# Summing the halves of an attention product in a later matmul, with another order on ScalarE and other steps for K

## The chip, the cores and the metric

The kernel runs on one core of one Trainium2 chip. The metric is the device time of one execution in microseconds (us), as a median over runs. The core's engines are TensorE (PE in the profile; PEld is its stream of weight loads), VectorE (DVE), ScalarE (ACT), GpSimd (POOL) and SyncE (SP), which here issues DMAs.

## What is computed

Three layers in a row, all in float32. The first is attention over pooled queries, the second a mixture of experts, the third a product with a cosine. The change lies in the first:

```
q, k, v: (2, 8, 1152, 64)
q_pool = q.reshape(B, H, S // 2, 2, D).mean(axis=3)
scores = scale * np.matmul(q_pool, k.transpose(0, 1, 3, 2))
scores = scores - np.max(scores, axis=-1, keepdims=True)
attn = np.exp(scores)
attn = attn / (np.sum(attn, axis=-1, keepdims=True) + 1e-09)
x = np.matmul(attn, v)          # then transposed to (1152 tokens, 512)
logits = x @ w_gate             # and x @ w_noise, top 2 of 8 experts
```

## The kernel before

Products of float32 are made from rounded high parts and the rest (low parts), as several matmuls of the type fp32r. The 8 heads are taken in 4 pairs (hp), a pair has two heads (hl), and a head has 9 tiles of 128 queries (t); over both batches these are 72 tiles, numbered n = 18 hp + 9 hl + t. In a tile, t = 4 holds queries of both batches.

The loop at L764 emits the work of all engines tile by tile, and each engine runs its own instructions in that order. In tile n:

- PE makes the scores of tile n + 1 in three banks of PSUM called s (s_mm, L285), from K tiles (kt, kb) and query tiles (q, l, qd).
- DVE reads the three maxima of n + 1 (s_max, L293), ACT the three exps (s_exp, L300), which write one tile p of three parts.
- PE transposes p of tile n in three groups (t_pe, L314) into banks called pt, of which there are three. ACT copies the first two as high parts eh (t_hi), DVE subtracts for the low parts el (t_lo). The third group ACT copies as it is to rw (t_pool, L339), and GpSimd makes eh and el of it.
- PE works off a queue of attention-value products (avq, L350): a group g of 2 or 3 token tiles (256 or 320 columns) takes 18 matmuls into the one bank pa. V stands in the weights as 64 high and 64 low columns, so rows 0 to 63 of pa hold the product with the high part, rows 64 to 127 that with the low part. NPOP (L761) says how many matmuls a tile takes; each group ends with the last of some tile.
- When a group has ended, fold_a (L367) lets ACT copy one half of pa to the other head's place, ft, and fold_b (L373) in the next tile, behind the first maximum, lets DVE add the other half to it: xt, with both heads of the pair, one below the other.
- For a pair's second head, fold_b also puts x_group (L606) in a list (fill). It is taken at the end of a tile that has no q_group or k_group: per token tile one matmul of xt with 160 columns of GW, an identity of 128 columns beside 32 columns of gate weights. That turns x token-major and gives its share of the logits. DVE then scales both (LGP, L620; X, L637), and SP writes X to memory (x_d, L640).

The steps of the next pair's K and Q are placed by plan (L642), a table of tile numbers: load_k, three k_group (PE transposes, ACT copies to st), k_split (GpSimd, high part sh and rest st) and k_asm (six DMAs from SP that put kt and kb together), each for both batches. m is the first tile of the pair ahead and d is 1 for the first such pair, else 0. The second batch of K is first needed by the scores of a pair's tile 4. SP issues its DMAs in order, so that one which waits holds up all behind it. At the start of a tile its planned steps come first, those of q_group and k_group last.

Behind the last tile come the rest of the products, the last x_groups and the routing of tokens (L842 ff.), then the experts.

Of the kernel before, what the change touches and what calls it, by code (L numbers as in the profile page):

```python
# [22 lines left out]
def attn_moe_cos_kernel(ctx, tc, q, k, v, w_gate, w_noise, noise, w1, w2, w_in, w_out, out):  # L23
# [27 lines left out]
    GW = xp.tile([128, 2, 192], F32, name="GW")  # L51
# [13 lines left out]
    def load_gate():  # L65
        nc.gpsimd.memset(GW, 0.0)
        for a in range(2):
            nc.gpsimd.tensor_scalar(GW[:, a, 32:160], ident, 1.0, 0.0, op0=OP.mult, op1=OP.add)
        for hl in range(2):
            rs = slice(hl * 64, hl * 64 + 64)  # L70
            for o in range(2):
                c = 160 * o + 16 * hl
                for i, w in enumerate((w_gate, w_noise)):
                    nc.sync.dma_start(GW[rs, :, c + 8 * i:c + 8 * i + 8],
                                      w.rearrange("(a o h d) e -> o h d a e", o=2, h=2, d=64)[o, hl])
# [238 lines left out]
    def t_pe(n, j):  # L314
        last = n == NTOT - 1 and j == 0
        TB[n, j] = p = ps.tile([128, 512], F32, name="s", bufs=4) if last else tbank()
        src = P[n].rearrange("p a b -> p (a b)")
        for i in range(3):
            c = 3 * j + i
            nc.tensor.transpose(p[:, i * 128:(i + 1) * 128], src[:, c * 128:(c + 1) * 128], ident)  # L320
# [25 lines left out]
    avq, fold, FT = [], [], {}  # L346
# [20 lines left out]
    def fold_a():  # L367
        hp, hl, g, p, w = fold[0]
        tmp = FT[0] = sb.tile([128, 320], F32, name="ft", bufs=2)
        me, ot = slice(hl * 64, hl * 64 + 64), slice(64 - hl * 64, 128 - hl * 64)  # L370
        nc.scalar.activation(tmp[me, 0:w], p[ot, 0:w], AF.Copy)

    def fold_b():  # L373
        hp, hl, g, p, w = fold.pop(0)
        b, lo, hi = GR[g]
        me = slice(hl * 64, hl * 64 + 64)
        if hl == 0 and g == 0:
            XT[hp] = sb.tile([128, N], F32, name="xt", bufs=1)
        nc.vector.tensor_tensor(XT[hp][me, lo:hi], p[me, 0:w], FT[0][me, 0:w], op=OP.add)  # L379
# [226 lines left out]
    def x_group(hp, g):  # L606
# [3 lines left out]
        lo, xo = (0, 32) if hp % 2 == 0 else (128, 0)  # L610
# [3 lines left out]
        pv = p[:, 0:160 * nt].rearrange("p (i c) -> p i c", c=160)  # L614
# [4 lines left out]
        def x_logits():  # L619
            nc.vector.tensor_tensor(LGP[:, ts, LGS[hp]:LGS[hp] + 2, :],  # L620
                                    pv[:, :, lo:lo + 32].rearrange("p i (h e) -> p i h e", h=2),
# [3 lines left out]
        x_mul = lambda: x_store(hp, ts, pv[:, :, xo:xo + 128], ri)  # L625
# [16 lines left out]
    def plan():  # L642
# [5 lines left out]
        for hp in range(HP):  # L648
# [6 lines left out]
            if hp:  # L655
# [108 lines left out]
    for n in range(NTOT):  # L764
# [57 lines left out]
        if fill and not fl:  # L822
# [21 lines left out]
    if avq:  # L844
        fold_a()
        fold_b()
# [4 lines left out]
    fold_a()  # L851
# [635 lines left out]
```

## Time and profile before

| what | value |
|---|---|
| three timed runs | 813.6, 813.65, 817.45 us, median 813.65 |
| the profiled execution | 812.25 us |
| its span, first to last instruction | 810.4 us |
| busy, share of the span | PE 94%, PEld 86%, DVE 77%, ACT 66%, POOL 49% |
| mean granted clock of PE | 0.977 |

The profile is of one execution. Busy shares are over the whole span; the attention takes the first 290 us or so, and its limits are read there. Times within the trace count from the span's start. A wait is put down to the engine that came last before it ended. PE and PEld are shown apart: matmuls run one behind the other and their ends are modelled, so a matmul record is longer than the step from one to the next.

### The profile page before, as it was taken

How to read it: one execution, taken by the hardware profiler on the slowest of the kernel's cores; microseconds unless marked ns; L12 is line 12 of the kernel's file. 1: busy time of each engine (PE TensorE's matmuls, PEld its weight loads, DVE VectorE, ACT ScalarE, POOL GpSimd, SP SyncE). 2: the span in 40 equal slices, each digit the busy share in tenths (PEclk: the TensorE clock that was granted, in tenths of full speed). 3: DMA queues.
4: the chain of work that ended last, by engine and by line, in shares of the span. 5: the costliest groups of instructions: out<-in, count | busy, mean ns of one | idle time of the engine just before them, and what ended most of it. 6: DMA issues, size and time to landing. Idle time of an engine off the chain costs nothing.

```text
span 810.4 us, 14005 instructions
## 1 busy us (share of the span) xinstructions
PE 765.7 (94%) x4915; PEld 700.7 (86%) x4915; DVE 627.7 (77%) x1240; ACT 534.4 (66%) x1257; POOL 397.1 (49%) x358
## 2 busy tenths in 40 slices
PE   7899999989999989899999999999978999999996
PEld 4699899979899879889999999999876899999995
DVE  5578878867888987459999999987689777685663
ACT  5799889869979884355555555645466666575553
POOL 4767777667867857406557656466055211000000
PEclk8999999999999999989999999999989999999999
DMA  9829769896864104977978979887433111000001
GB/s 206 180 64 201 179 155 240 222 243 138 205 136 143 59 8 170 326 230 246 322 253 308 317 257 337 275 311 225 169 100 116 53 53 27 30 24 28 1 0 43
DMA packets 90141, 133.64 MB, mean 165 GB/s; under 512 B 26928, under 2 KB 57008, under 8 KB 90064
## 3 DMA queue, kind: packets, MB, share of 16 engines
q1 hardware_dynamic: 83664, 111.17, 48.9%
q0 software_dynamic: 5392, 18.48, 6.3%
q10 hardware_dynamic: 1008, 3.02, 1.4%
q8 instruction: 41, 0.67, 0.3%
q14 instruction: 36, 0.29, 0.1%
HBM read 81.20 MB, written 29.88 MB: 137 GB/s over the span
## 4 chain that ended last, share of the span: by engine, by line
PE 58%; DVE 13%; DMA 9%; ACT 8%; issue 5%; POOL 5%; SPq 0%; ACTq 0%; DVEq 0%; POOLq 0%
PE h L977 19%; PE acc L977 12%; PE acc L1008 7%; PE pa L358 6%; PE s L280 6%; PE pt L320 5%; DMA kt<-st 4%; ACT p L304 3%; DVE u L563 2%; DMA qn<-in_q_dram 1%; POOL xg_d L529 1%; ACT u L562 1%; PE t L969 1%; DVE cn L1297 1%; POOL st L227 1%
## 5 line engine op out<-in xcount | busy, mean ns | idle before, releaser
L296 DVE TENSOR_REDUCE nm<-s 128x1 f32<-128x384 f32 x216 | 110.4, 550 | 48.0 <-PE s L280 32.3
L304 ACT ACTIVATE p<-s,nm 128x384 f32<-128x384 f32 x216 | 123.7, 584 | 10.1 <-DVE nm L298 8.8
L977 PE MATMUL h<-xe,u 128*128 128x320 f32 x768 | 126.0, 313 | 0.0
L977 PEld LDWEIGHTS h<-xe,u 128*128 128x128 f32 x768 | 114.1, 188 | 2.1
L1064 POOL TENSOR_SCALAR raw<-raw 128x1024 f32<-128x1024 f32 x16 | 66.0, 4124 | 94.5 <-ACT raw L1063 90.2
L563 DVE TENSOR_TENSOR u<-raw,u 128x1024 fp32r<-128x1024 f32 x66 | 88.7, 1348 | 19.7 <-ACT u L562 19.5
L320 PE MATMUL pt<-ident,p 128*128 128x128 f32 x645 | 98.9, 278 | 1.9 <-ACT rw L341 1.1
L280 PE MATMUL s<-kt,q 128*128 128x384 f32 x240 | 84.2, 371 | 10.5 <-DMA kt<-st 6.4
L358 PE MATMUL pa<-eh,v 128*128 128x320 f32 (+1 forms) x279 | 87.9, 330 | 1.6 <-DVE xt L379 0.9
L320 PEld LDWEIGHTS pt<-ident,p 128*128 128x128 f32 x645 | 78.3, 142 | 10.8 <-ACT rw L341 5.8
L977 PE MATMUL h<-x,u 128*128 128x256 f32 (+1 forms) x576 | 87.0, 302 | 0.0
L977 PEld LDWEIGHTS h<-x,u 128*128 128x128 f32 x576 | 83.4, 195 | 3.7 <-DVE cr L1304 0.4
L562 ACT ACTIVATE u<-raw 128x1024 fp32r<-128x1024 f32 x73 | 76.8, 1057 | 8.1 <-DMA raw<-w_d 5.0
L358 PE MATMUL pa<-el,v 128*128 128x320 f32 (+1 forms) x279 | 81.5, 307 | 0.0
L333 ACT ACTIVATE eh<-pt 128x384 fp32r<-128x384 f32 x144 | 63.3, 494 | 24.9 <-PE pt L320 23.7
L1008 PE MATMUL acc<-hh,u 128*128 128x320 f32 x448 | 76.4, 313 | 0.0
L337 DVE TENSOR_TENSOR el<-pt,eh 128x384 fp32r<-128x384 f32 x144 | 73.3, 549 | 2.7 <-ACT eh L333 1.0
L344 POOL TENSOR_TENSOR el<-rw,eh 128x384 fp32r<-128x384 f32 x71 | 71.7, 1011 | 5.9
L1008 PEld LDWEIGHTS acc<-hh,u 128*128 128x128 f32 x448 | 68.7, 190 | 0.1
L977 PE MATMUL acc<-u,gh 128*128 128x512 f32 x216 | 68.6, 399 | 0.0
L343 POOL TENSOR_SCALAR eh<-rw 128x384 fp32r<-128x384 f32 x71 | 36.4, 512 | 65.4 <-ACT rw L341 58.8
L1082 POOL DMA_INDIRECT g<-y_d,ROWC x18 | 20.3, 1129 | 96.8 <-DVE cm L1090 67.5
(237 smaller groups left out, 1719.7 us busy)
## 6 DMA issues: line engine op xcount, KB each, us to landing
raw<-in_moe_w_dram SPq DMA_DIRECT2D x64, 512.0 KB, 5.9
raw<-in_moe_w_in_dram SPq DMA_DIRECT2D x16, 512.0 KB, 4.6
raw<-in_moe_w_out_dram SPq DMA_DIRECT2D x16, 512.0 KB, 7.2
w_d<-dw POOLq DMA_DIRECT2D x16, 512.0 KB, 6.5
raw<-w_d SPq DMA_DIRECT2D x14, 512.0 KB, 4.2
xg_d<-ZERO SPq DMA_DIRECT2D x10, 512.0 KB, 5.9
vn<-in_v_dram SPq DMA_DIRECT2D x16, 288.0 KB, 5.0
q<-sh SPq DMA_DIRECT2D x14, 304.0 KB, 4.4
```

The lines of the kernel that those rows point to most:

```text
L280: nc.tensor.matmul(o, l, r, start=(m == 0), stop=(not lo and m == len(mm) - 1))
L296: nc.vector.tensor_reduce(NM[n][:, i:i + 1], SB[n][i][:, 0:384], axis=AX.X, op=OP.max, negate=True)
L304: nc.scalar.activation(P[n][:, i], SB[n][i][:, 0:384], AF.Exp, bias=NM[n][:, 3:4], accum_out=SUMS[:, t, 2 * hp + hl, i:i + 1])
L320: nc.tensor.transpose(p[:, i * 128:(i + 1) * 128], src[:, c * 128:(c + 1) * 128], ident)
L337: nc.vector.tensor_tensor(el, t_src(n, j), ef, op=OP.subtract)
L344: nc.gpsimd.tensor_tensor(el, rw, ef, op=OP.subtract)
L358: nc.tensor.matmul(st["p"][:, 0:w], V2[hp, hl, b][:, c, :], (EH, EL)[s][:, c, EB[g]:EB[g] + w], start=(c == 0 and s == 0), stop=(c == 8 an ...
L562: nc.scalar.activation(b[:, 0], r, AF.Copy)
L563: st_w["lo"].tensor_tensor(b[:, 1], r, b.bitcast(F32)[:, 0], op=OP.subtract)
L977: nc.tensor.matmul(o, l, r, start=first and i == 0, stop=last and i == len(seq) - 1)
L1008: nc.tensor.matmul(ACC[e, d][:, 0:CAP], w[:, i, 128 * d:128 * d + 128], r, start=f == 0 and r is hh and i == 0, stop=f == 7 and r is hl)
L1064: nc.gpsimd.tensor_scalar(m, m, 2.0 ** -15, 0.0, op0=OP.is_ge, op1=OP.add)
```

## The change

- fold_a and fold_b become one step, fold_x: DVE copies all 128 rows of pa to xt, a tile of its own for each head (two buffers), in the same tile n, behind t_lo. ACT copies no ft any more. The step stands before the tile's x_group, so a group can now be folded and turned in one tile.
- x_group makes two matmuls per token tile, one for each head, of 80 columns. GW holds the 64-wide identity twice, in rows 0 to 63 and 64 to 127, so that the matmul adds the halves; the gate weights stand twice too.
- p is three tiles of four buffers in place of one of two. ACT's rw comes before the third exp.
- K: the second and third k_group of the first batch, its split, load and assembly, and the third k_group of the second batch, its split and assembly come one tile earlier (for the first such pair only those of the second batch).
- In the last tile no x_group is taken from the list.

```diff
-    GW = xp.tile([128, 2, 192], F32, name="GW")
+    GW = xp.tile([128, HP, 96], F32, name="GW")
...
     def load_gate():
-        nc.gpsimd.memset(GW, 0.0)
-        for a in range(2):
-            nc.gpsimd.tensor_scalar(GW[:, a, 32:160], ident, 1.0, 0.0, op0=OP.mult, op1=OP.add)
...
+        for hp in range(HP):
+            for h in range(2):
+                c = slice(64 * h, 64 * h + 64)
+                nc.gpsimd.tensor_scalar(GW[c, hp, 16:80], ident[c, c], 1.0, 0.0, op0=OP.mult, op1=OP.add)
...
         if i == 0:
-            P[n] = sb.tile([128, 3, 384], F32, name="p", bufs=2)
-        nc.scalar.activation(P[n][:, i], SB[n][i][:, 0:384], AF.Exp, bias=NM[n][:, 3:4],
+            P[n] = []
+        P[n].append(sb.tile([128, 384], F32, name="p", bufs=4))
+        nc.scalar.activation(P[n][i], SB[n][i][:, 0:384], AF.Exp, bias=NM[n][:, 3:4],
...
-    def fold_a():
-        hp, hl, g, p, w = fold[0]
-        tmp = FT[0] = sb.tile([128, 320], F32, name="ft", bufs=2)
-        me, ot = slice(hl * 64, hl * 64 + 64), slice(64 - hl * 64, 128 - hl * 64)
-        nc.scalar.activation(tmp[me, 0:w], p[ot, 0:w], AF.Copy)
-
-    def fold_b():
+    def fold_x():
         hp, hl, g, p, w = fold.pop(0)
         b, lo, hi = GR[g]
-        me = slice(hl * 64, hl * 64 + 64)
-        if hl == 0 and g == 0:
-            XT[hp] = sb.tile([128, N], F32, name="xt", bufs=1)
-        nc.vector.tensor_tensor(XT[hp][me, lo:hi], p[me, 0:w], FT[0][me, 0:w], op=OP.add)
+        if g == 0:
+            XT[hp, hl] = sb.tile([128, N], F32, name="xt", bufs=2)
+        nc.vector.tensor_copy(XT[hp, hl][:, lo:hi], p[:, 0:w])
         if hl == 1:
             fill.append(lambda: x_group(hp, g))
...
         for i, t in enumerate(tl):
-            nc.tensor.matmul(p[:, 160 * i:160 * i + 160], XT[hp][:, t * 128:(t + 1) * 128],
-                             GW[:, hp // 2, 32 - xo:192 - xo], start=True, stop=True)
...
+            for hl in range(2):
+                c = 160 * i + 80 * hl
+                nc.tensor.matmul(p[:, c:c + 80], XT[hp, hl][:, t * 128:(t + 1) * 128],
+                                 GW[:, hp, 16 * hl:16 * hl + 80], start=True, stop=True)
...
                 for j in range(3):
-                    at(m + (8 + d, 10, 11)[j], k_group, hp, 0, j)
-                at(m + 12, k_split, hp, 0)
-                at(m + 12, load_k, hp, 1)
-                at(m + 13, k_asm, hp, 0)
+                    at(m + (8 + d, 9 + d, 10 + d)[j], k_group, hp, 0, j)
+                at(m + 11 + d, k_split, hp, 0)
+                at(m + 11 + d, load_k, hp, 1)
+                at(m + 12 + d, k_asm, hp, 0)
                 for j in range(3):
-                    at(m + (14, 15, 17)[j], k_group, hp, 1, j)
-                at(m + 18, k_split, hp, 1)
-                at(m + 19, k_asm, hp, 1)
+                    at(m + (14, 15, 16)[j], k_group, hp, 1, j)
+                at(m + 17, k_split, hp, 1)
+                at(m + 18, k_asm, hp, 1)
...
         if nx:
             s_mm(n + 1)
-            s_max(n + 1, 0)
-        if fold:
-            fold_b()
-        if nx:
-            s_max(n + 1, 1)
-        if nx:
-            s_max(n + 1, 2)
+            for i in range(3):
+                s_max(n + 1, i)
...
         if fold:
-            fold_a()
+            fold_x()
         if nx:
+            t_pool(n, 2)
             s_exp(n + 1, 2)
-            t_pool(n, 2)
...
-        if fill and not fl:
+        if fill and not fl and nx:
             fill.pop(0)()
```

Three places show how the instructions move. The first is PE in tile n = 12, where the product of the first token group of a pair's second head ends; rows are in PE's order, s are scores of the next tile, GW the matmuls of x_group. Before:

```order
L358 MATMUL pa<-el,v_606 128x256
L280 MATMUL s<-kt,q_279 128x384
L280 MATMUL s<-kt,l_282 128x384
L280 MATMUL s<-kt,q_279 128x384
L280 MATMUL s<-kt,l_282 128x384
L280 MATMUL s<-kt,q_279 128x384
L280 MATMUL s<-kt,l_282 128x384
L320 MATMUL pt<-ident,p 128x128 x9
L612 MATMUL pa<-GW,xt 128x160 x2
```

Now:

```order
L358 MATMUL pa<-el,v_623 128x256
L606 MATMUL pa<-GW,xt 128x80 x4
L280 MATMUL s<-kt,q_281 128x384
L280 MATMUL s<-kt,l_284 128x384
L280 MATMUL s<-kt,q_281 128x384
L280 MATMUL s<-kt,l_284 128x384
L280 MATMUL s<-kt,q_281 128x384
L280 MATMUL s<-kt,l_284 128x384
L320 MATMUL pt<-ident,p 128x128 x9
```

The matmuls of x_group stand directly behind the product that they read, a tile earlier. The same holds in eight places in all: for the first token group of each pair, for the last one of the first three pairs, and for the second one of the last pair.

The second place is SP's queue where the third pair of heads begins (n = 36), with the DMAs that put together the second batch of K. Before:

```order
L640 DMA x_d<-X 128x2x128
L154 DMA l_2348<-ql 64x1216 x2
L162 DMA qd<-ql 64x128 x2
L425 DMA xg_d<-ZERO 128x2x512
L640 DMA x_d<-X 128x3x128
L237 DMA kt<-sh 64x1152
L239 DMA kb<-sh 64x1152
L240 DMA kt<-st 64x1152
```

Now:

```order
L634 DMA x_d<-X 128x2x128
L154 DMA l_2416<-ql 64x1216 x2
L162 DMA qd<-ql 64x128 x2
L237 DMA kt<-sh 64x1152
L239 DMA kb<-sh 64x1152
L240 DMA kt<-st 64x1152
```

The pieces of kt stand ahead of the write of X of the third token group (128x3x128), and directly behind l and qd. The write of X ahead of these is that of the second group, whose x_group is now taken one tile later.

The third place is ACT in two tiles of the attention in which a k_group is copied (st). Before, with a fold in the second of them:

```order
L333 ACTIVATE eh<-pt 128x3x128 x2
L304 ACTIVATE p,SUMS<-s,nm 128x384 x2
L371 ACTIVATE ft<-pa 64x256
L304 ACTIVATE p,SUMS<-s,nm 128x384
L341 ACTIVATE rw<-pt 128x384
L171 ACTIVATE st<-pt 128x384
```

Now:

```order
L333 ACTIVATE eh<-pt 128x3x128 x2
L305 ACTIVATE p,SUMS<-s,nm 128x384 x2
L341 ACTIVATE rw<-pt 128x384
L305 ACTIVATE p,SUMS<-s,nm 128x384
L171 ACTIVATE st<-pt 128x384
```

The copy to ft is gone, and rw stands before the third exp.

## Rows read from the trace of the kernel before

**Rows 1.** Busy time by stretch: from:to, length, PE, PEld, DVE, ACT, POOL, PEclk, DMA share, GB/s.

```profile
90.00:120.00 30.00, 28.54 (x204) 26.42 (x203) 23.68 (x56) 26.15 (x82) 23.52 (x26) 1.00 0.80 194
...
150.00:180.00 30.00, 26.38 (x179) 24.70 (x178) 21.39 (x53) 22.16 (x66) 20.17 (x25) 0.94 0.97 230
180.00:210.00 30.00, 29.67 (x217) 28.39 (x217) 23.53 (x57) 28.44 (x87) 21.84 (x24) 1.00 0.76 168
```

**Rows 2.** Waits, 35 to 290 us: engine, line <- waited for: us in total, times, longest.

```profile
PEld s L280 <- ACT p L304: 6.5, 21, 0.5
PEld pt L320 <- ACT rw L341: 5.8, 17, 0.6
...
PE s L280 <- DMA kt<-st: 4.7, 3, 3.3
...
PEld pt L612 <- DVE el L337: 1.4, 3, 0.5
PE pt L320 <- ACT rw L341: 1.1, 4, 0.4
...
PE s L280 <- ACT p L304: 0.9, 5, 0.2
PE pa L358 <- DVE xt L379: 0.9, 2, 0.6
...
PE pt L612 <- DVE el L337: 0.8, 3, 0.3
PE pa L358 <- DVE X L637: 0.7, 1, 0.7
```

**Rows 3.** The chain that ended last, 150 to 173 us: start, us, what.

```profile
164.34 7.12 DMA kt<-st
...
171.60 1.44 PE s L280 x6
```

**Rows 4.** Busy time by stretch behind that wait, columns as in rows 1.

```profile
172.00:174.00 2.00, 2.00 (x11) 1.90 (x10) 1.39 (x3) 0.00 (x0) 1.75 (x3) 0.66 0.95 208
174.00:176.00 2.00, 2.00 (x11) 2.00 (x10) 1.47 (x4) 1.50 (x5) 0.00 (x0) 0.50 1.26 250
```

**Rows 5.** SP's DMA issues, 150 to 173 us: start, us, queue, line, what, count.

```profile
153.70 0.37 SPq L640 DMA_DIRECT2D x_d<-X  x1
...
155.32 2.39 SPq L162 DMA_DIRECT2D qd<-ql  x2
...
161.86 0.37 SPq L640 DMA_DIRECT2D x_d<-X  x1
162.33 1.27 SPq L237 DMA_DIRECT2D kt<-sh  x1
```

**Rows 6.** Groups of instructions by line and form: count | busy us, mean ns | idle before.

```profile
L379 DVE TENSOR_TENSOR xt<-pa,ft 64x320 f32<-64x320 f32 x16 | 7.7, 484 | 0.3
L371 ACT ACTIVATE ft<-pa 64x320 f32<-64x320 f32 x17 | 7.3, 432 | 0.7 <-PE pa L358 0.3
...
L379 DVE TENSOR_TENSOR xt<-pa,ft 64x256 f32<-64x256 f32 x15 | 6.3, 418 | 0.8 <-ACT ft L371 0.5
...
L1018 DVE COPY yt<-acc 128x320 f32<-128x320 f32 x14 | 6.1, 476 | 0.5 <-PE acc L1008 0.5
```

**Rows 7.** Weight loads in order of time, 84 us: start, us, what, count.

```profile
84.10 0.19 PEld L358 LDWEIGHTS pa<-eh,v 128*128 128x128 f32 x1
84.21 0.19 PEld L358 LDWEIGHTS pa<-el,v 128*128 128x128 f32 x1
...
84.80 0.61 PEld L612 LDWEIGHTS pt<-GW,xt 128*128 128x128 f32 x4
```

**Rows 8.** Matmuls in order of time at the end of a product, 70 us: columns as in rows 7.

```profile
70.19 0.28 PE L358 MATMUL pa<-el,v 128*128 128x256 f32 x1
70.31 0.33 PE L280 MATMUL s<-kt,q 128*128 128x384 f32 x1
```

**Rows 9.** DVE in order of time behind the x_group of that product: columns as in rows 7.

```profile
74.56 0.41 DVE L637 TENSOR_TENSOR X<-pa,RINV 128x256 f32<-128x256 f32 x1
```

More of the change, by code (lines that the diff above doesn't have):

```diff
@@ L65, in load_gate @@
     def load_gate():
-        nc.gpsimd.memset(GW, 0.0)
-        for a in range(2):
-            nc.gpsimd.tensor_scalar(GW[:, a, 32:160], ident, 1.0, 0.0, op0=OP.mult, op1=OP.add)
[L69 to L72, printed above, removed]
+        for hp in range(HP):
+            for h in range(2):
+                c = slice(64 * h, 64 * h + 64)
+                nc.gpsimd.tensor_scalar(GW[c, hp, 16:80], ident[c, c], 1.0, 0.0, op0=OP.mult, op1=OP.add)
+        for half in range(2):
+            rs = slice(half * 64, half * 64 + 64)
+            for h in range(2):
                 for i, w in enumerate((w_gate, w_noise)):
-                    nc.sync.dma_start(GW[rs, :, c + 8 * i:c + 8 * i + 8],
-                                      w.rearrange("(a o h d) e -> o h d a e", o=2, h=2, d=64)[o, hl])
+                    c = 80 * h + 8 * i
+                    nc.sync.dma_start(GW[rs, :, c:c + 8], w.rearrange("(a h d) e -> h d a e", h=2, d=64)[h])
     QB1 = 640
@@ L316, in t_pe @@
         TB[n, j] = p = ps.tile([128, 512], F32, name="s", bufs=4) if last else tbank()
-        src = P[n].rearrange("p a b -> p (a b)")
         for i in range(3):
-            c = 3 * j + i
-            nc.tensor.transpose(p[:, i * 128:(i + 1) * 128], src[:, c * 128:(c + 1) * 128], ident)
+            c = slice(i * 128, i * 128 + 128)
+            nc.tensor.transpose(p[:, c], P[n][j][:, c], ident)
     def t_dst(n, j):
@@ L344, in t_pool @@
         nc.gpsimd.tensor_tensor(el, rw, ef, op=OP.subtract)
-    avq, fold, FT = [], [], {}
+    avq, fold = [], []
     fill = []
@@ L609, in x_group @@
         p = tbank() if g else ps.tile([128, 512], F32, name="pa", bufs=1)
-        lo, xo = (0, 32) if hp % 2 == 0 else (128, 0)
         for i, t in enumerate(tl):
-            nc.tensor.matmul(p[:, 160 * i:160 * i + 160], XT[hp][:, t * 128:(t + 1) * 128],
-                             GW[:, hp // 2, 32 - xo:192 - xo], start=True, stop=True)
-        pv = p[:, 0:160 * nt].rearrange("p (i c) -> p i c", c=160)
+            for hl in range(2):
+                c = 160 * i + 80 * hl
+                nc.tensor.matmul(p[:, c:c + 80], XT[hp, hl][:, t * 128:(t + 1) * 128],
+                                 GW[:, hp, 16 * hl:16 * hl + 80], start=True, stop=True)
+        pv = p[:, 0:160 * nt].rearrange("p (i k c) -> p i k c", k=10, c=16)
         hs = slice(2 * hp, 2 * hp + 2)
@@ L620, in x_logits @@
             nc.vector.tensor_tensor(LGP[:, ts, LGS[hp]:LGS[hp] + 2, :],
-                                    pv[:, :, lo:lo + 32].rearrange("p i (h e) -> p i h e", h=2),
+                                    pv[:, :, 0:10:9],
                                     ri.to_broadcast([128, nt, 2, 16]), op=OP.mult)
             logits(hp, ts)
-        x_mul = lambda: x_store(hp, ts, pv[:, :, xo:xo + 128], ri)
+        x_mul = lambda: x_store(hp, ts, pv[:, :, 1:9].rearrange("p i k c -> p i (k c)"), ri)
         if hp == HP - 1 and g > 1:
@@ L844, in attn_moe_cos_kernel @@
     if avq:
-        fold_a()
-        fold_b()
+        fold_x()
     pump(ra, 1)
@@ L850, in attn_moe_cos_kernel @@
         avq.pop(0)()
-    fold_a()
+    fold_x()
     pump(ra, 2)
-    fold_b()
     for t in range(3):
```

## The prediction

> **What bounds the kernel now.** I read first the busy time by stretch [rows 1]. Up to some 290 us the kernel runs its 72 attention tiles, and behind them the change touches only the last products. In an ordinary stretch TensorE (PE) is busy for 29.67 of 30 us and ScalarE (ACT) for 28.44, so PE sets the pace with ACT close behind; in the stretch from 150 us PE loses more than 3 us and its clock falls. A busy PE is not a PE at its peak, so next come the waits of that stage [rows 2]. PE's matmuls stand 4.7 us for the K tiles (kt), nearly all in one wait of 3.3; the rest are many short waits for ACT and VectorE (DVE). The matmul stream (PE) and the weight-load stream (PEld) give each cause twice: the first is a lower bound of what it costs, the second an upper one, since a load that waits may still be in time. Third I read the chain around the long wait [rows 3], the clock behind it [rows 4] and the DMA queue of SyncE (SP) ahead of it [rows 5].
>
> The sum is made against the profiled execution, 812.25 us (its span is 810.4), which lies 1.4 below the median of the three timed runs, 813.65. I put the difference that the sum gives on the median. A run of this kernel tells about 0.5%, 4.1 us, from no change.
>
> **K one tile earlier: −5.2 us.** The wait for kt is 3.3 us for the third pair of heads and 4.7 for all three pairs [rows 2]. With K's second half split and assembled one tile earlier, GpSimd's part is out of the way some 4 us sooner. But the pieces also stand in SP's queue. There the write of X (x_d), the pieces l and the pieces qd stand ahead of them, and x_d of this place now belongs to the second group of tokens, whose x_group has moved from the second-last to the last tile of the pair, because a k_group took its tile. In the trace this x_d is issued at 153.70 and the next, two tiles on, at 161.86 [rows 5]: 4.1 us per tile. So it goes out at about 157.8. With l and qd the queue then takes until 157.71 − 153.70 = 4.0 us later, 161.8, where the first kt piece went out at 162.33 before. The whole shift of kt is thus 0.5 us and not 4: kt<-st is issued at 163.8 and, with the 7.12 us that it took [rows 3], lands at 171.0. PE asked for it at 171.60 − 3.3 = 168.3, and by the costs below it now asks some 2 us later. About 1.2 of the 3.3 stays, the 1.4 of the other two goes (4.7 − 3.3, both covered by half a microsecond earlier and two later): 3.5 saved. Behind the long wait PE's clock was at 0.66 of full speed for 2 us and at 0.50, its lower level of 1.2 GHz, for 2 more [rows 4]; before that it stood idle. The two other waits together were 1.4 us, and the stretch of the first of them, from 90 us, has a clock of 1.00 [rows 1]; so I expect none behind 1.2 us and take 2 × 0.34 + 2 × 0.50 = 1.7 as saved. The bounds of the two are 0 and 6.4.
>
> **ACT's order and the copies that go: −5.4 us.** The 32 copies of half the product (ft) leave ACT: 17 of 0.432 us [rows 6] are 7.3 us, and the narrower ones come on top. rw now stands before the third exp, so its PSUM bank (pt) comes free one exp sooner. What waits for rw is PE's next transposes, between 1.1 us (matmul stream) and 5.8 (load stream) [rows 2]; each such wait is at most 0.6, so I expect them to go and take the middle, 3.4. PE's score matmuls wait for the exps between 0.9 and 6.5 us [rows 2]; the exps do not get shorter, ACT only arrives sooner, so I take 2.0, nearer the lower end. The third exp is later by a copy, but its transposes come behind two others and four products on PE: nothing, and at most that copy's 0.4 us in a tile where they are not enough.
>
> **The sum taken by the copy: −3.1 us.** DVE adds with one operand in PSUM in 0.418 us for 256 columns; a copy of 320 from PSUM took 0.476 and the addition 0.484 [rows 6], so the copy costs what the addition did. It is no longer held behind a row maximum of the next tile, so the bank pa is free before the next product starts: the waits of the products for xt (0.9) and for X (0.7) go, 1.6. The wait of x_group for el, between 0.8 and 1.4 [rows 2], goes with its old place: 1.1. In the tail one copy leaves the chain on ACT: 0.4.
>
> **What the matmul now costs: +4.9 us.** Before, 36 matmuls of 160 columns; now 72 of 80. Ten and twenty of these lie in the tail, where PE then waits for the routing anyway. In the tiles 31 become 62, and as each shows as two records, 62 records become 124. Four loads of the old form took 0.61 us, the last 0.19 of it: one per 0.14 [rows 7], 8.7 us in all. The new ones stream half the columns but load weights just as wide. The nearest rows are two such loads with nothing to hold them, which start 0.11 apart (84.10 and 84.21) [rows 7]; I take 0.11, as the load then sets the pace: 13.6 us, so +4.9. If streaming set it, it would be 0.07, half of 0.14, and the cost nothing.
>
> **The new wait: +5.6 us.** In eight places x_group now stands directly behind the product that it reads: for the first group of tokens of all four pairs, for the last group of three, and for the second of the last pair. PE must wait there until DVE has copied. The last product starts at 70.19 and takes 0.28, and the next matmul went at 70.31 [rows 8]. With the copy of 0.42 to 0.48 PE starts 0.28 + 0.43 − 0.12 = 0.6 us later, and two hand-overs come on top; a landing took 0.14 to its matmul (171.46 to 171.60) [rows 3]. I take 0.7, eight times. Behind it PE holds back the next tile's scores, and DVE its maxima. Below: 0 where ACT was late in any case. Above: the second rival.
>
> GpSimd's new steps for the gate weights, three more tiles for p and one more for xt cost nothing: the gate is read a head later, and the buffers only loosen waits.
>
> **Sum:** −3.5 − 1.7 − 5.4 − 3.1 + 4.9 + 5.6 = −3.2, so 813.65 − 3.2 = **810.4 us**, 0.4% faster: too little to tell from no change.
>
> **The rivals.**
> The first, faster: ACT was the true pace. Then all waits for it go, 5.8 + 6.5 instead of 5.4, 6.9 us more: 803.5. For it speaks ACT's 28.44 of 30 us [rows 1], against it that the matmul stream itself shows only 1.1 and 0.9 of these waits [rows 2].
>
> The second, slower: DVE's chain becomes the bound. After the copy DVE waits for x_group's matmuls (now eight records, 0.88 us), then multiplies X (0.41 [rows 9]) and the logits, and only then reads the next tile's three maxima. The exps of that tile start about 1.1 us later than before (copy 0.42, 0.88 − 0.56 = 0.32 more of matmuls, and the 0.41 that stood behind the maxima before). PE loses this wherever the products left in the queue do not cover it, above all for the first group, behind which the queue is empty for one tile. If all eight places lose it in full, that is 8.8: 819.2. It decides from the point where half of them do, since then nothing of the gain is left.
>
> The third, faster: weights load behind the running matmul so that the narrow ones cost 0.07 each. Then the 4.9 goes: 805.5. Against it stands the 0.11 [rows 7]. The Trainium skill (TensorE: Matmul & The Clock Gate, Back-to-back issue gap) gives some 81 ns for a load and its matmul of 128 columns; by that, an estimate from the page, the 124 records take 10.0 us instead of 13.6 and the time is 806.9. No row here shows a pair of such loads as fast.
>
> The fourth, that the change does not do what it says: kt stays as late, as its queue's first piece moves by only 0.5 us. Then the 3.5 and 1.7 are not saved: 815.6, no change.
>
> **How the numbers follow.** My forecast 0.48, its own range 807 to 814; the first rival 0.18, the second 0.14, the third 0.12, the fourth 0.08. Faster by over 0.5% (under 809.6) are the first, the third and a quarter of my own case: 0.42. Slower (over 817.7) are the second and a trace of mine: 0.15. The rest, 0.43, is no change. The range that leaves out 2 in 10 reaches from the first rival to the fourth, 803.5 to 815.6; the second and a part of the first lie outside.
>
> **What would show it.** K: the longest wait for kt between 0.5 and 2 us, no stretch at half clock in the attention, and kt's first piece issued directly behind qd. ACT: waits for rw near 0. Matmul: weight loads of x_group 0.11 apart. New wait: eight waits of PE for xt, 0.6 to 0.8 each. Wrong would be a wait for kt above 3 us or none at all, loads 0.07 apart, or waits of PE for exps that grow behind the eight places; a change behind 320 us, where no line is touched, would upset the whole argument.

## The result

The changed kernel takes 821.84 us (median of nine runs, 817.53 to 824.6) against 814.61 of the kernel before (nine runs, 811.94 to 819.14): ratio 1.0073, 95% interval 1.0046 to 1.01. It is slower by 0.7%, above the range of the prediction and near the second rival's 819.2. The profiled execution took 823.1 us, its span is 821.3, the mean clock 0.974.

**Where the time went.** I mark each of the 72 tiles by the start of its first exp. First come the marks of tiles 5 and 71, from ScalarE in order of time (start, us, line, operation, in brackets the idle time before it), before and then after:

```profile
38.98 0.58 ACT L304 ACTIVATE p<-s,nm 128x384 f32<-128x384 f32 x1
...
289.06 0.58 ACT L304 ACTIVATE p<-s,nm 128x384 f32<-128x384 f32 x1 [0.32 <-DVE nm L298]
```

```profile
40.71 0.58 ACT L305 ACTIVATE p<-s,nm 128x384 f32<-128x384 f32 x1
...
296.26 0.58 ACT L305 ACTIVATE p<-s,nm 128x384 f32<-128x384 f32 x1 [0.43 <-DVE nm L298]
```

From tile 5 to 71 it is 250.08 us before and 255.55 after: +5.5, where the medians are 7.2 apart and the two profiled executions 10.9. The start up to tile 5 took between 36.7 and 40.9 us in the profiles of all the kernels below, and what lies behind tile 71 between 518.8 and 526.0, in no order that goes with the edits; so I read them as spread between executions and compare only the 66 tiles between. I split these by the same marks into three sums of stretches, which together are the whole:

- **ordinary**: tiles 5 to 13, 23 to 31, 41 to 49, 59 to 67 (32 tiles, nothing but the tiles' own work);
- **first groups**: 13 to 18, 31 to 36, 49 to 54, 67 to 71 (x_group of a pair's first group of tokens, and what follows);
- **K**: 18 to 23, 36 to 41, 54 to 59 (a pair's start: l, qd, the second half of K, the later groups).

| us | ordinary | first groups | K | tile 5 to 71 |
|---|---|---|---|---|
| before | 115.8 | 71.4 | 63.0 | 250.1 |
| after | 112.0 | 74.9 | 68.7 | 255.6 |
| difference | −3.7 | +3.5 | +5.7 | +5.5 |

The ordinary tiles became faster, as meant. The loss stands where x_group was moved ahead and, the larger part, where the steps for K were.

The waits of the changed kernel, 35 to 298 us (engine, line <- waited for: us in total, times, longest), answer to [rows 2]:

```profile
PEld s L280 <- ACT p L305: 7.3, 15, 1.4
...
PE s L280 <- ACT p L305: 3.0, 5, 1.1
PE s L280 <- DMA kt<-st: 3.0, 2, 1.9
PEld pa L606 <- DVE xt L372: 2.9, 4, 0.7
PE pt L606 <- DVE el L337: 2.5, 3, 0.8
...
PE pa L606 <- DVE xt L372: 2.1, 4, 0.5
...
PE pt L606 <- DVE xt L372: 1.4, 4, 0.4
```

No wait for rw is left. The wait for kt is 3.0, longest 1.9. PE's waits for exps rose from 0.9 to 3.0, longest 1.1 where it was 0.2: the sign that I had named for the second rival. The stretches of [rows 1], and behind the long kt wait those of [rows 4], in the changed kernel (columns as there):

```profile
90.00:120.00 30.00, 27.48 (x203) 25.86 (x202) 23.63 (x57) 22.25 (x69) 19.98 (x24) 1.00 0.86 213
150.00:180.00 30.00, 26.70 (x192) 25.59 (x191) 22.30 (x55) 20.07 (x60) 22.11 (x25) 0.97 0.79 202
180.00:210.00 30.00, 30.00 (x221) 29.28 (x220) 23.84 (x58) 27.98 (x86) 19.14 (x23) 0.97 0.87 199
```

```profile
177.00:179.00 2.00, 1.74 (x8) 1.77 (x9) 1.08 (x2) 0.00 (x0) 1.84 (x3) 0.81 1.01 222
179.00:181.00 2.00, 2.00 (x11) 1.90 (x10) 1.19 (x3) 0.85 (x2) 0.00 (x0) 0.50 1.01 331
```

PE is busy a microsecond less from 90 us than before, and there is still a stretch at half clock behind the wait for kt.

**Behind the first group.** PE in order of time at the first such place of the changed kernel:

```profile
71.07 0.28 PE L358 MATMUL pa<-el,v 128*128 128x256 f32 x1
71.87 1.12 PE L606 MATMUL pa<-GW,xt 128*128 128x80 f32 x8 [0.52 <-DVE xt L372]
72.78 0.42 PE L280 MATMUL s<-kt,q 128*128 128x384 f32 x1
```

From the product's last matmul to the next scores it is 72.78 − 71.07 = 1.71 us, where it was 0.12 [rows 8]: 0.8 until x_group starts and 0.91 for its eight records.

**At the pair's start.** VectorE and then GpSimd of the changed kernel, from 91 us. L595 to L597 are r_inv, a step that no edit touches: it sums a group's sums of exps, adds 1e-9 and takes the reciprocal.

```profile
91.88 0.15 DVE L595 TENSOR_REDUCE RINV<-SUMS 128x4 f32<-128x12 f32 x1
92.07 1.91 DVE L596 TENSOR_SCALAR RINV<-RINV 128x4 f32<-128x4 f32 x1
94.01 0.18 DVE L597 RECIPROCAL RINV<-RINV 128x4 f32<-128x4 f32 x1
...
94.22 0.41 DVE L631 TENSOR_TENSOR X<-pt,RINV 128x256 f32<-128x256 f32 x1
94.55 1.48 DVE L296 TENSOR_REDUCE nm<-s 128x1 f32<-128x384 f32 x3
```

```profile
91.31 2.64 POOL L227 TENSOR_TENSOR st<-st,sh 128x1152 f32<-128x1152 f32 x1
```

The addition on 128x4 numbers takes 1.91 us and ends at 93.98, when GpSimd's subtraction for K (in k_split) ends, at 93.95. X and the next maxima stand behind it, and SP's queue behind X. SP's issues there, of the kernel before and of the changed one:

```profile
86.26 0.38 SPq L640 DMA_DIRECT2D x_d<-X  x1
86.73 1.26 SPq L154 DMA_DIRECT2D l<-ql  x2
88.05 2.38 SPq L162 DMA_DIRECT2D qd<-ql  x2
94.43 0.38 SPq L640 DMA_DIRECT2D x_d<-X  x1
94.91 0.46 SPq L237 DMA_DIRECT2D kt<-sh  x1
```

```profile
94.66 0.38 SPq L634 DMA_DIRECT2D x_d<-X  x1
95.14 1.16 SPq L154 DMA_DIRECT2D l<-ql  x2
96.35 2.44 SPq L162 DMA_DIRECT2D qd<-ql  x2
98.89 0.54 SPq L237 DMA_DIRECT2D kt<-sh  x1
```

Before, l went out 8.2 us and qd 6.9 us ahead of kt. Now X's write holds all three, and they go out one behind the other, l 8.4 us later than before (the tiles stand 2.3 later: tile 18's mark is at 90.25, before at 87.91).

### The profile page after: what moved, and what is told of

The parts are those of the page before. It is cut to its first block, busy times and chain, and to the rows that moved or that the text cites. A ratio compares the mean times of both kernels' runs of the same rounds, so it can differ in the third digit from the quotient of the medians.

```text
span 821.3 us, 14118 instructions
## 1 busy us (share of the span) xinstructions
PE 772.3 (94%) x4987; PEld 711.6 (87%) x4987; DVE 627.5 (76%) x1240; ACT 519.8 (63%) x1224; POOL 395.5 (48%) x363
## 4 chain that ended last, share of the span: by engine, by line
PE 69%; DVE 12%; DMA 6%; ACT 5%; issue 4%; POOL 2%; SPq 1%; ACTq 0%; DVEq 0%; POOLq 0%
PE h L964 20%; PE acc L964 11%; PE acc L995 8%; PE s L280 7%; PE pa L358 7%; PE pt L320 7%; DMA kt<-st 3%; DVE u L556 2%; PE pt L854 1%; DVE cn L1284 1%; PE t L956 1%; ACT u L555 1%; PE t L1011 1%; DVE hl L975 1%; DMA raw<-in_moe_w_out_dram 1%
## 5 line engine op out<-in xcount | busy, mean ns | idle before, releaser
L296 DVE TENSOR_REDUCE nm<-s 128x1 f32<-128x384 f32 x216 | 107.6, 549 | 41.5 <-PE s L280 27.0
L964 PE MATMUL h<-xe,u 128*128 128x320 f32 x768 | 128.4, 316 | 2.6 <-issue 2.5
L305 ACT ACTIVATE p<-s,nm 128x384 f32<-128x384 f32 x216 | 125.6, 589 | 7.1 <-DVE nm L298 6.2
L320 PE MATMUL pt<-ident,p 128*128 128x128 f32 x645 | 95.4, 277 | 1.3 <-ACT st L171 0.6
L333 ACT ACTIVATE eh<-pt 128x384 fp32r<-128x384 f32 x144 | 63.2, 491 | 47.9 <-PE pt L320 46.6
L343 POOL TENSOR_SCALAR eh<-rw 128x384 fp32r<-128x384 f32 x71 | 36.4, 513 | 70.8 <-ACT rw L341 56.0
L995 PEld LDWEIGHTS acc<-hh,u 128*128 128x128 f32 x448 | 68.7, 190 | 1.9 <-issue 1.8
```

The lines of the kernel that those rows point to most:

```text
L296: nc.vector.tensor_reduce(NM[n][:, i:i + 1], SB[n][i][:, 0:384], axis=AX.X, op=OP.max, negate=True)
L305: nc.scalar.activation(P[n][i], SB[n][i][:, 0:384], AF.Exp, bias=NM[n][:, 3:4], accum_out=SUMS[:, t, 2 * hp + hl, i:i + 1])
L320: nc.tensor.transpose(p[:, c], P[n][j][:, c], ident)
L964: nc.tensor.matmul(o, l, r, start=first and i == 0, stop=last and i == len(seq) - 1)
L995: nc.tensor.matmul(ACC[e, d][:, 0:CAP], w[:, i, 128 * d:128 * d + 128], r, start=f == 0 and r is hh and i == 0, stop=f == 7 and r is hl)
```

## The experiments

All were timed beside the kernel before. The theory from the first reading has two parts: x_group, directly behind its product, makes exps late, and the steps for K are caught in SP's queue. The table gives medians, ratios to the kernel before as it was timed beside each, and the stretches (us) of one profile each.

| kernel | median us | ratio, 95% interval | ordinary | first groups | K | 5 to 71 |
|---|---|---|---|---|---|---|
| x_next_tile | 812.51 | 0.9985 (0.9961 to 1.001) | 112.0 | 65.7 | 69.9 | 247.7 |
| k_alone | 813.1 | 0.999 (0.9962 to 1.0017) | 115.9 | 69.8 | 67.2 | 252.9 |
| act_alone | 812.39 | 0.9974 (0.9946 to 1.0002) | 114.0 | 72.2 | 62.7 | 248.9 |
| narrow_alone | 812.4 | 0.9987 (0.9962 to 1.0012) | 115.9 | 71.6 | 63.2 | 250.7 |
| x_next_xd_late | 801.97 | 0.9865 (0.9825 to 0.9904) | 112.0 | 66.0 | 63.3 | 241.2 |
| k_xd_late | 812.15 | 0.9996 (0.9973 to 1.002) | 115.8 | 69.8 | 63.5 | 249.1 |
| dve_behind | 821.54 | 1.0094 (1.0061 to 1.0128) | 112.1 | 73.3 | 74.2 | 259.5 |
| k_undone | 813.03 | 1.0004 (0.9979 to 1.0028) | 112.0 | 77.9 | 62.6 | 252.5 |
| x_behind_scores | 812.26 | 0.9979 (0.9947 to 1.0012) | 112.1 | 68.7 | 66.6 | 247.4 |
| after_xd_late | 813.31 | 0.999 (0.9967 to 1.0013) | 112.1 | 74.0 | 63.7 | 249.8 |
| before_xd_late | 808.57 | 0.9924 (0.9896 to 0.9952) | 116.0 | 71.6 | 58.3 | 245.8 |
| best_k_undone | 803.22 | 0.9838 (0.9795 to 0.9882) | 112.2 | 68.0 | 59.1 | 239.2 |
| after_no_add | 809.69 | 0.9982 (0.9962 to 1.0001) | 112.1 | 74.9 | 64.3 | 251.3 |
| best_no_add | 798.96 | 0.9843 (0.9816 to 0.987) | 112.0 | 65.2 | 59.3 | 236.5 |
| best_k_undone_no_add | 798.08 | 0.9855 (0.9822 to 0.9889) | 112.2 | 66.9 | 58.9 | 238.0 |
| before_no_add | 808.53 | 0.9947 (0.9919 to 0.9976) | 115.0 | 70.8 | 62.6 | 248.4 |

**x_group in the next tile** (x_next_tile):

```diff
+        nf = len(fill)
         if fold:
             fold_x()
...
-        if fill and not fl and nx:
+        if nf and not fl and nx:
```

> The changed kernel, with x_group taken no sooner than the tile after its product (as the kernel before took it); all else as changed. Theory: x_group directly behind its product makes VectorE's chain (copy, wait for x_group, X, next maxima) and with it the exps late, some 1.1 us in most of eight places: the time falls by 8 to 10 us, to 812 to 814, and the waits of the x_group matmuls for xt and the longest waits for exps behind them go. Rival A (the narrow matmuls cost the loss): stays within 2 us of 821.8. Rival B (ScalarE's new order makes the exps late): stays within 2 of 821.8. Rival C (instructions are supplied late behind 320 us, because the program is longer): stays within 2 of 821.8, and the loss lies behind 310 us.

The time fell to 812.51. The first groups lose 9.2 us and end below the kernel before; the K stretches do not gain (69.9, from 68.7). PE at the same place in this kernel:

```profile
70.72 0.28 PE L358 MATMUL pa<-el,v 128*128 128x256 f32 x1
70.83 0.33 PE L280 MATMUL s<-kt,q 128*128 128x384 f32 x1
...
71.90 1.15 PE L320 MATMUL pt<-ident,p 128*128 128x128 f32 x9
72.88 1.02 PE L606 MATMUL pa<-GW,xt 128*128 128x80 f32 x8
73.69 0.42 PE L280 MATMUL s<-kt,q 128*128 128x384 f32 x1
```

In the next tile the queue of products is empty: nine transposes, then x_group, with no wait. Rivals A to C fall.

**Parts of the change, each alone in the kernel before** (k_alone: the hunk of plan; act_alone and narrow_alone as follows):

```diff
+        P[n].append(sb.tile([128, 384], F32, name="p", bufs=4))
...
-            s_exp(n + 1, 2)
             t_pool(n, 2)
+            s_exp(n + 1, 2)
```

```diff
-            nc.tensor.matmul(p[:, 160 * i:160 * i + 160], XT[hp][:, t * 128:(t + 1) * 128],
-                             GW[:, hp // 2, 32 - xo:192 - xo], start=True, stop=True)
+            for k in range(2):
+                c, o = 160 * i + 80 * k, 32 - xo + 80 * k
+                nc.tensor.matmul(p[:, c:c + 80], XT[hp][:, t * 128:(t + 1) * 128],
+                                 GW[:, hp // 2, o:o + 80], start=True, stop=True)
```

> The kernel before with the new steps for K alone. Theory: saves most of the 4.7 us of waits for kt and the 1.7 of low clock, less some 0.5 for an x_group that is moved one tile: 810 to 812. Rival D (kt is no earlier, as X's write and the pieces l and qd stand ahead of it in SyncE's queue): within 1 us of 814.6, and the wait for kt stays over 3 us.

> The kernel before with p as three tiles and rw ahead of the third exp alone; the copies of half the product stay. Theory: the waits of transposes for rw go (1.1 to 5.8 us), the exps are not missed: 810 to 813. Rival B (the third exp, later by a copy, holds the transposes, or the earlier rw makes nothing earlier): 815 to 820, with waits of PE for p that grow by more than the waits for rw shrink.

> The kernel before with each 160-column matmul of x_group as two of 80 columns with the same weights; all else as before. Theory: the loads set the pace at 0.11 us each, 62 more records of them in the attention less the halved streaming: +4 to +5, 818.5 to 819.5. Rival A (they cost more, since VectorE waits for x_group and the maxima wait for VectorE): 820 to 823. Rival E (loads are hidden behind other work, or fall where PE waited anyway): 814 to 816.

K alone: no gain that can be measured, 4.2 us more in its own stretches, and a longest wait for kt of 2.6; nearer Rival D than the theory. ACT's order alone: inside what the theory gave, at the edge of what can be measured, 1.7 us in the ordinary tiles. The narrow matmuls: no cost that can be measured (Rival E), 0.6 us in the 66 tiles where I had put 4.9. PE at x_group in the kernel before, then in narrow_alone, shows why:

```profile
72.69 0.71 PE L612 MATMUL pa<-GW,xt 128*128 128x160 f32 x4
73.13 0.45 PE L280 MATMUL s<-kt,q 128*128 128x384 f32 x1
...
73.94 0.44 PE L280 MATMUL s<-kt,q 128*128 128x384 f32 x1 [0.19 <-ACT p L304]
```

```profile
74.08 1.02 PE L614 MATMUL pa<-GW,xt 128*128 128x80 f32 x8
74.89 0.42 PE L280 MATMUL s<-kt,q 128*128 128x384 f32 x1
...
75.32 0.44 PE L280 MATMUL s<-kt,q 128*128 128x384 f32 x1
```

The narrow form takes 0.81 us to the next scores (74.89 − 74.08) where the wide one took 0.44. But the second bank's scores start 1.24 us behind x_group's start, and before it was 1.25: PE waited there for the exps anyway.

**SP's queue, the place of DVE's work, K undone.** In x_next_xd_late and k_xd_late X's write is put in a list and issued two tiles later; dve_behind puts VectorE's multiplications for X and the logits behind the next tile's maxima; k_undone takes the old lines of plan.

```diff
-        nc.sync.dma_start(x_d.rearrange("(t p) d -> p t d", p=128)[:, ts, hp * 128:(hp + 1) * 128], xo)
+        dst = x_d.rearrange("(t p) d -> p t d", p=128)[:, ts, hp * 128:(hp + 1) * 128]
+        xdq.append((at_n[0] + 2 if at_n[0] < 1000 else 0, lambda: nc.sync.dma_start(dst, xo)))
...
+        at_n[0] = n
+        xd_flush()
```

```diff
-            x_logits()
-            x_mul()
...
+            xd.extend((x_logits, x_mul))
...
             for i in range(3):
                 s_max(n + 1, i)
+        while xd:
+            xd.pop(0)()
```

> The changed kernel with x_group in the tile after its product, and X's write (x_d) issued two tiles later than X is computed, so that SyncE's queue never stands for it; the new steps for K stay. Theory: with K one tile earlier, l, qd and kt are held by x_d, which waits for x_group: the stretches of tiles 18 to 23, 36 to 41 and 54 to 59 lose the 3.0, 1.5 and 2.5 us that they gained against the kernel before, and the kt waits shrink below 2 us in all: 804 to 808. Rival F (the DMA engines are the limit there; the pieces take 7 us to land whenever they go out): 811 to 813, kt waits stay near 4 us.

> The kernel before with the new steps for K and with X's write issued two tiles later; nothing else. Theory: what the steps for K were meant to save appears once nothing stands ahead of kt in SyncE's queue: 807 to 810, kt waits under 2 us in all, the stretch of tiles 18 to 23 back at about 20 us or less. Rival F: as the steps for K alone, 812 to 814.

> The changed kernel with x_group where the change puts it, directly behind its product, but with VectorE's multiplications of the logits and X put behind the next tile's three maxima. PE still waits for the copy. Theory: the exps are late through VectorE's chain (copy, wait for x_group, X, then the maxima); with the maxima free of it most of the loss goes: 813 to 816. Rival G (PE's wait for the copy, 0.7 us eight times, is the loss, as it holds the scores back): 819 to 822, 813 to 816 not reached.

> The changed kernel with the steps for K as before. Theory: the steps for K bring nothing here and move an x_group whose write of X then holds l, qd and kt, so that undoing them saves 2 to 5 us: 817 to 820. Rival H (they save what was forecast, 5 us, and the loss elsewhere is that much larger): 825 to 828.

x_next_xd_late: 801.97, below what the theory gave; its K stretches lose 6.7 us and no wait for kt is left. k_xd_late missed: no gain over k_alone in the time (its K stretches fall by 3.7, and no wait for kt is left). In its trace ScalarE stands 3.71 us ahead of the exps of tile 20, and in k_alone 2.00 at the same place:

```profile
99.51 0.47 ACTq L84 DMA_DIRECT2D qn<-in_q_dram  x1
100.03 0.87 ACT L333 ACTIVATE eh<-pt 128x384 fp32r<-128x384 f32 x2 [3.71 <-DMA kb<-sh]
```

```profile
92.85 1.73 ACTq L84 DMA_DIRECT2D qn<-in_q_dram  x2
94.62 0.87 ACT L333 ACTIVATE eh<-pt 128x384 fp32r<-128x384 f32 x2 [2.00 <-DMA l<-ql]
```

Each time an issue of ScalarE's own, a load of Q (qn), comes straight before this eh, and it is the issue that waits. In the trace a DMA counts its landing on a semaphore, and each of these issues first waits on the very one on which it will count. The issue at 99.51 shares its semaphore with kb<-sh, which SP had issued at 91.64 and whose last part landed at 99.48: of the 3.71 us, 3.2 are this wait. In k_alone the second of the two issues, at 94.11, shares its own with l<-ql, landed at 94.08: of the 2.00 us, 0.8 are this wait and 1.0 the two issues themselves. What it costs in time was not tried by a run.

dve_behind gained nothing; part of that is a cost of the edit itself, as x_group's bank pt is held longer (PE waits 7.5 us for X in six places). At tile 32, where the bank is pa, the answer is clean: from the mark of tile 31 to that of tile 32 it takes 1.65 us more than in x_next_tile, and in the changed kernel 1.71 more. So it is not VectorE's work ahead of the maxima. DVE of dve_behind at the first place shows the maxima ahead of X and still late, for the scores:

```profile
73.15 1.49 DVE L296 TENSOR_REDUCE nm<-s 128x1 f32<-128x384 f32 x3 [1.60 <-PE s L280]
...
74.88 0.41 DVE L630 TENSOR_TENSOR X<-pa,RINV 128x256 f32<-128x256 f32 x1
```

k_undone: 813.03, a larger gain than expected, though its first groups take 3.1 us longer than the changed kernel's (ScalarE waits three times, 5.0 us in all, to write st until the DMA kt<-st has read it). Inside the change the steps for K cost some 0.7% (1.0073 less 1.0004).

**Ahead of or behind the scores, and the queue without the rest.**

```diff
             for i in range(3):
                 s_max(n + 1, i)
+        while xl:
+            xl.pop(0)()
...
-            fill.pop(0)()
+            xl.append(fill.pop(0))
```

after_xd_late and before_xd_late have the edit of SP's queue above in the two kernels; best_k_undone is x_next_xd_late with the old lines of plan.

> The changed kernel with x_group put behind the next tile's scores instead of ahead of them: the same tile of products, the same copy, the matmuls one step further on in PE's order. Theory: what costs is that x_group, its wait of 0.7 and its 0.9 us of matmuls, stands ahead of the next tile's scores in a tile in which PE has no slack; behind them the exps of that tile are not late and most of the 9 us is back: 812 to 816, and the tiles behind the first group lose under 0.5 us instead of 1.7. Rival I (the place in the tile does not matter; it is the work of x_group in a full tile): 818 to 822.

> The changed kernel with X's write issued two tiles later; x_group stays directly behind its product. Theory: SyncE's queue no longer holds l, qd and kt; the three stretches of tiles 18 to 23, 36 to 41 and 54 to 59 get back 5 to 8 us, the loss behind the first groups stays: 813 to 817. Rival F (the queue's order is not what holds kt): 820 to 823.

> The kernel before with X's write issued two tiles later; the steps for K as before. Theory: in the kernel before, X's write stands ahead of kt too (issued 0.48 us before it), but K's preparation ends only then, so little is won: within 3 us of 812.6. Rival J (X's write alone was what held kt): 806 to 809.

> The fastest so far (x_group in the next tile, X's write two tiles later) with the steps for K as before. Theory: with SyncE's queue free, K one tile earlier is worth the kt waits of the kernel before, 3 to 5 us: 805 to 808 without it. Rival K (the steps for K are worth nothing even then, the gain is the queue's alone): 801 to 803.

x_behind_scores has the time of x_next_tile. At tile 32 its exps are 0.85 us late against x_next_tile, where in the changed kernel it was 1.71: half of the loss of a place is x_group's matmuls in a tile without slack, half is PE standing for the copy ahead of the scores (x_group's records take 0.91 us, and PE stood 0.8 for the copy). (The edit also puts X's write behind the steps of K in SP's queue, and no wait for kt is left, so not all of its gain is the scores'.) after_xd_late: 813.31, its K stretches at 63.7. Its queue, from 84 us:

```profile
84.28 1.98 SPq L154 DMA_DIRECT2D l<-ql  x2
...
90.02 0.46 SPq L237 DMA_DIRECT2D kt<-sh  x1
...
98.25 0.38 SPq L635 DMA_DIRECT2D x_d<-X  x1
```

l goes out 10.9 us sooner than in the changed kernel (the mark of tile 18 stands 1.2 sooner). before_xd_late gained 0.76%, as Rival J had it, and its waits for kt fell to 1.7: the kernel before paid for X's write too. best_k_undone is level with x_next_xd_late: with the queue free the steps for K are worth nothing (Rival K).

**The small addition.** Without X's write in the way, x_next_xd_late still had K stretches longer by 4.2 us than best_k_undone, and additions of 1.9 to 2.2 us.

```diff
         nc.vector.tensor_reduce(ri, SUMS[:, ts, hs, :], axis=AX.X, op=OP.add)
-        nc.vector.tensor_scalar(ri, ri, 1e-9, None, op0=OP.add)
         nc.vector.reciprocal(ri, ri)
```

> The changed kernel without the addition of 1e-9 to the sums of the exps in r_inv (the sums are at least 1, so that the 1e-9 is below their last bit); it leaves this addition out. In the trace of the changed kernel that addition (128x4) takes 1.87 to 1.91 us in three places, 0.17 elsewhere, and ends when GpSimd's subtraction for K's second half (k_split, 2.64 us) ends; with the steps for K one tile earlier this subtraction lies beside the r_inv of the last group. Theory L: this holds VectorE's X and the next maxima and so the exps of tiles 19, 37 and 55, 1.7 us each: 816 to 818. Rival F (X's write in SyncE's queue alone costs there): 820 to 823.

> The kernel with x_group in the next tile, X's write two tiles later and the steps for K of the change, without the addition of 1e-9 (left out). Theory L: its three long additions (1.9 to 2.2 us) go, 802.0 less 4 to 6: 796 to 798. Rival M (the reciprocal, or another VectorE instruction, then stands for GpSimd instead): 801 to 803, with reciprocals of over 1 us in the same places.

> As the run with x_group in the next tile, X's write two tiles later and the steps for K as before, without the addition of 1e-9 (left out). Its long additions were 0.46 us only, three of them. Theory L: 803.2 less 0 to 1.5, so 802 to 803, and thus 4 to 6 behind the same kernel with the new steps for K: those are worth their 4 us only without the addition. Rival M: both kernels without the addition within 1.5 us of each other.

> The kernel before without the addition of 1e-9 (left out). In its trace the addition is long in three other places (1.44, 1.22 and 1.07 us, at 219.6, 267.1 and 278.3 us). Theory L: 0 to 3 us saved, 810 to 813. Rival M: within 1 us of before, 812.6 to 814.6.

after_no_add takes 809.69, below the 816 to 818 of the theory. Its marks are free of a step at just the named tiles: against it the changed kernel is later by 1.75 us at tile 19, 1.71 at 37, 1.71 at 55, and the other steps are within 0.25 up to tile 18 and, but for tiles 22, 23, 40 and 41, where kt arrives, behind it. The 66 tiles give 4.2 us; the ratios give 1.0073 − 0.9982, 0.9%, some 7 us with intervals of about 2 us each. DVE of after_no_add at the place:

```profile
88.08 0.18 DVE L596 RECIPROCAL RINV<-RINV 128x4 f32<-128x4 f32 x1
```

The reciprocal does not take the addition's place as the one that stands: it lies beside GpSimd's subtraction, which runs there from 87.20 to 89.85, and takes 0.18 us. best_no_add gained 3 us over x_next_xd_late in the medians, less than the 4 to 6 expected, and only 0.2% in the ratios, which is inside their intervals; in the 66 tiles it is 4.7 us, and the steps to tiles 19, 37 and 55 are shorter by 1.9, 1.8 and 2.0. best_k_undone_no_add missed: it is level with best_no_add, as Rival M had it (the theory wanted 4 to 6 between them), and in the 66 tiles 1.4 apart: here the steps for K are worth about a microsecond. before_no_add gains 0.5%, a little above the theory; 1.7 us of it lie in the 66 tiles. The two fastest, 798.96 and 798.08, beat the kernel before by 1.4 to 1.6% and the changed one by more than 2%.

## Why the prediction was wrong, point by point

**K one tile earlier, −5.2: wrong.** The step that failed is "The whole shift of kt is thus 0.5 us and not 4", with "at about 157.8". I saw that X's write stands ahead of kt, and moved it by one tile. SP's queue of the changed kernel at that pair:

```profile
164.19 0.37 SPq L634 DMA_DIRECT2D x_d<-X  x1
...
169.61 1.15 SPq L240 DMA_DIRECT2D kt<-st  x1
```

X's write is issued 10.5 us later than before (153.70); tile 36's mark is 4.5 later, so that x_d moved by 6.0 us: one tile, and the 1.87 us that the addition took there, which now ran beside GpSimd's subtraction. kt<-st was issued at 164.34 before [rows 3], so against the tiles it goes out 0.8 us later and not 0.5 sooner. I had written GpSimd's part as "out of the way some 4 us sooner", and not asked what stands beside it at its new place. The queue also held l and qd, which I had only counted as length. kt's waits fell from 4.7 to 3.0 where I had 1.2 left, and the half clock stayed: −1.7 in place of −3.5, and 0 of the 1.7. The long wait is 1.9 where it was 3.3, inside the 0.5 to 2 that I had named as a sign, but only because PE asks for kt 2.5 us later against the tiles (at 175.35 where it was 168.35). The sum had such a delay in it, from its other terms; it is no gain of the steps for K, and that the sign came true was luck. (By the sum's own numbers, landed at 171.0 and asked for at 170.3, 0.7 should have stayed and not 1.2.) Against all that stand some 1.7 us at each of three tiles for the addition. Undone, the steps gave back 0.7%.

Of the two causes only the addition tells the two kernels apart. X's write in SP's queue costs both nearly the same: taking it away is worth 0.8% in each, and some 5 us of the K stretches in each. Without the addition the K stretches fall by 4.4 us in the changed kernel and by 0.4 in the kernel before. So the queue is a reason why the steps for K save little, and the addition is the larger part of what they cost.

**The new wait, 8 × 0.7 = +5.6: its size was near, its place wrong.** The waits are 2.1 in four places and 1.4 in four, 3.5 on the matmul stream (2.9 and 2.0, so 4.9, on the loads). The step that failed here is the one that priced the wait alone, "PE must wait there until DVE has copied", and the matmuls apart from their place: x_group's own 0.91 us came out of a tile in which PE waits for exps anyway and went into one full of products, ahead of the next scores. So behind a first group the next scores start 1.6 us later (1.71 where it was 0.12) and not 0.7. Moving x_group back gave 0.9% (1.0073 to 0.9985).

**The narrow matmuls, +4.9: wrong at the old place.** Loads are 0.11 apart, as forecast: eight records take 0.91. But "the load then sets the pace" holds only where PE does; alone they cost 0.6 us in 66 tiles. (The tail holds five of the old matmuls and ten of the new; the "ten and twenty" of the sum are their records, and its 31 and 62 are right.) The third rival, loads 0.07 apart, falls; that they would be covered by the wait for exps was no rival of mine.

**ACT's order and copies −5.4, the sum by DVE −3.1: right in kind.** rw's waits are gone. The order alone gave 1.7 us in the ordinary tiles. best_k_undone differs from before_xd_late by x_group's matmuls, the sum and ACT's part only: 239.2 against 245.8 us, −6.6. The sum's terms for it, −5.4 − 3.1 + 4.9, were −3.6; with the narrow matmuls at the measured 0.6 they are −7.9.

**Put together.** By the ratios x_group's place is worth +0.88% and the steps for K +0.69%; what is left of the change is −0.86% (best_k_undone, 0.9838, against before_xd_late, 0.9924). The three add up to +0.71%, and measured are +0.73%; each ratio has an interval of some 0.3% to either side. Of 814.6 us they are +7.2, +5.6 and −7.0, and with the narrow matmuls (0.6) taken from the last to the first, x_group cost 7.8 where its two terms were +10.5, ACT's order and the sum by the copy gave −7.6 where theirs were −8.5, and K cost 5.6 where it was to give −5.2. So K is the term on which the forecast failed; that x_group's cost as a whole came out no larger than forecast is luck, as one of its two terms was too large and the other too small.

**The rivals.** The second came nearest in time, 819.2, and its sign, growing waits for exps, was there. Its mechanism is not what happened: with the maxima ahead of X (dve_behind) the exps of tile 32 are as late, because the scores are. The fourth (kt stays late) is part of the truth. The first was right that exps pace the old x_group tiles. A change behind 320 us, which would have upset the argument, cannot be told from the spread between executions. PE does stand there for 7.4 us, between 320 and 345 us, in the profile of the changed kernel, for nothing that the profile shows, and in that of the kernel before it does not. But in act_alone it stands 6.2 us, and in k_undone and dve_behind, which have the changed kernel's number of instructions within ten, not at all. So it goes with no one edit, and what it is stays open.

**What stays open.** Why the steps for K bring next to nothing even with the queue free and the addition gone: best_k_undone_no_add still waits 2.2 us for kt and best_no_add not at all, but their 66 tiles are only 1.4 us apart and their times level. And how much of k_alone's loss is ScalarE's issue of qn.

## What to carry to other kernels

Before a filler is moved, look at whether its engine has slack at the old place and at the new one: the same eight matmuls cost nothing that could be measured in a tile that waits for exps, and 0.9 us plus a wait ahead of the next scores in a full one. In a queue that is worked off in order, a write that waits for late data belongs behind the loads that are due sooner; issuing X's write two tiles later was worth 0.8% in the kernel before and 0.8% in the changed one. When a long GpSimd step is moved, look at which small VectorE instruction then runs beside it and what stands behind that.

## What was not expected of the hardware

A VectorE addition of a constant on 128x4 numbers in SBUF lasts until the GpSimd instruction beside which it starts has ended. All sixteen of the changed kernel (count: shortest, median, longest in ns):

```profile
L596 DVE TENSOR_SCALAR RINV<-RINV x16: 169/170/1908, 64.5 to 301.2; 128x4 f32<-128x4 f32 x12, 128x6 f32<-128x6 f32 x4
```

Three are 1.87 to 1.91 us, and each ends 0.02 to 0.03 us behind GpSimd's subtraction, which was running when it started. Three of the other thirteen have a GpSimd instruction start 0.02 to 0.03 us behind their own start, and do not stretch. In the fourteen kernels with the addition, before and after among them, 86 of 224 take longer than 0.175 us, up to 2.24, and every one ends 0.02 to 0.03 us behind a GpSimd instruction. The sums of exps and the reciprocals on the same numbers do not stretch: in the changed kernel none takes more than 0.17 and 0.20 us, beside GpSimd or not. The Trainium skill (SBUF — State Buffer, SBUF: two separate sides) says that VectorE and GpSimd share a pair of ports which one of them holds for a whole instruction, VectorE where it runs in a mode that uses two ports; by that rule an addition in such a mode waits for the subtraction, and the trace agrees with such a wait: the addition started 0.76 us into a GpSimd instruction of 2.64 and lasted the other 1.91. No run here shows which mode the addition ran in.

The second surprise is that ScalarE, too, was held by DMAs that SP had issued: its own issue of a load stood until a DMA on the same semaphore had landed, 3.2 us in k_xd_late and 0.8 in k_alone, and went out 0.03 us behind that landing both times.
